# Attention followed by a gated MLP: an earlier start of the first v tiles, a check of the softmax sums on the chip, and a branch at the end

## The chip, the core and the metric

The kernel runs on one core of one Trainium2 chip. The core has five engines that work side by side and meet at semaphores: TensorE (PE in the profile, with PEld for its weight loads), VectorE (DVE), ScalarE (ACT), GpSimd (POOL) and SyncE (SP), which here issues transfers. Sixteen DMA engines move data between the memory of the chip (DRAM) and the core's on-chip memory SBUF. [...] The metric is the device time of one execution in microseconds; the kernel before takes 251.71 us (median of three runs, 251.39 to 252.03).

## The reference

Per batch (8 of them), grouped-query attention with 16 query heads, 4 key and value heads, 384 positions and head size 64, and then a gated MLP with a spatial gate on its result:

```python
k = np.repeat(k, group, axis=1); v = np.repeat(v, group, axis=1)
scores = scale * np.matmul(q, k.transpose(0, 1, 3, 2))
scores = scores - np.max(scores, axis=-1, keepdims=True)
attn = np.exp(scores)
attn = attn / (np.sum(attn, axis=-1, keepdims=True) + 1e-09)
x = np.matmul(attn, v)          # then to (B, S, 1024)
...
h = np.maximum(x @ w_in, 0.0)   # (1024, 1024)
u, v = h[..., :512], h[..., 512:]
v_n = (v - mean(v)) / np.sqrt(var(v) + 1e-06)
v_s = np.einsum('ts,bsd->btd', w_spatial, v_n) + b_spatial[None, :, None]
out = (u * v_s) @ w_out         # (512, 1024)
```

The inputs q, k and v are normal numbers times 0.1, so that scores are small; the kernel before computes exp without subtracting the maximum.

## The kernel before

The whole program is written out without loops on the chip; the order of each engine's queue is the order in which Python calls the helpers. The outer loop counts turns n from 0 to 149. A batch has 18 *units* (NU): six groups m (three tiles of 128 query rows, two halves of the heads), each with three tiles of 128 keys. `scores(n)` (L224) makes two matmuls of 512 columns into a double-buffered PSUM tile `sc` and one exp on ScalarE (L240), which casts to the fp16 tile `aT`. When the three units of a group are done, `weigh` (L242) makes, for each of the two key heads of the half, twelve matmuls of 65 columns into the single PSUM buffer `av`; the 65th column is the sum of the softmax, because `v1` carries a column of ones. VectorE takes the reciprocal `r` (L257) and multiplies (L259) into `x16`. Two `weigh` calls of a group stand in neighbouring turns, and the second needs the buffer that the first one's multiplication frees.

x is transposed into `xt`: in batch 0, and for the last two groups of the last batch, on TensorE by `x_transposes` (L271, with a copy on VectorE), else by a transposing transfer on SP's queue. The MLP runs as *fill*: a generator `stream` (L467) yields after each matmul the columns it spent, and `run_fill` (L631) draws as many columns as the turn is allotted (L651 to L657). Its pieces are `v_tile` (L288: eight matmuls of 512 columns, then `vr`, `stats` and `mv` on VectorE), `u_tile` or `u_block`, `normal` (L311), `gate`, and `project`. All of these, the transposes and the warm matmuls share the three PSUM buffers with the tag `ck`.

`normal` makes rstd on ScalarE (L314, L315: Ln, then Exp), `nmr` = -mean x rstd on VectorE (L316), and the three normalised tiles `vn` = vr x rstd + nmr, mostly on POOL (L327). `keep_warm` (L545) makes small matmuls on the identity while little other work is there: 27 at the very start, some between the first transposes, and four in each of the turns 0 to 9, 14 and 15. Their PSUM tile `warm` (L543) is held from the start until turn 15.

The turns at which casts, transfers and transposes stand are written out by hand (`at`, `turn_at`). Within a turn the order is: listed loads and casts, scores, `weigh`, listed transposes and warm matmuls, fill. Up to turn 16 each turn n makes the scores of unit n + 1; from turn 18 on each even turn makes two units.

At the end the last batch's `project` sends each half row block on its own (L462), the last in two pieces of 384 and 128 columns. Then follows the framework's closing block (L684): SP waits for every transfer, and all engines meet at a barrier twice.

Of the kernel before, what the change touches and what calls it, by code (L numbers as in the profile page):

```python
# [17 lines left out]
def kernel(  # L18
# [166 lines left out]
    def k_transposes(b, j, eng):  # L185
        ps = ps_ck.tile([P, S], FP16, name=f"kps_{b}_{j}", tag="ck")
        for t in range(NT):
            nc.tensor.transpose(
                ps[:, t * P : (t + 1) * P],
                k16s[b][:, j, t].rearrange("p h d -> p (h d)"),  # L190
                ident16,
            )
        eng(k_tile(b)[:, j], ps)
# [25 lines left out]
        )  # L219


    aTs, avs, x16s, xts = {}, {}, {}, {}

    def scores(n):  # L224
# [17 lines left out]
    def weigh(b, m, hh):  # L242
        qt, j = divmod(m, 2)
        av = ps_av.tile([P, G, D + 1], FP32, name=f"av_{b}_{m}_{hh}", tag="av")
        for i in range(G):
            for t in range(NT):
                nc.tensor.matmul(  # L247
                    av[:, i, :],
                    aTs[b, m][:, t, hh, i * P : (i + 1) * P],
                    v1[b % 2][:, 2 * j + hh, t, 0 : D + 1],  # L250
                    start=(t == 0),
                    stop=(t == NT - 1),
                )
# [3 lines left out]
        nc.vector.reciprocal(r, av[:, :, D : D + 1])  # L257
        blk = 4 * j + 2 * hh
        nc.vector.tensor_tensor(  # L259
            x16s[b][:, qt, blk : blk + 2].rearrange("p k (i d) -> p (k i) d", i=2),  # L260
            av[:, :, 0:D],
            r.to_broadcast([P, G, D]),
            ALU.mult,
        )
# [6 lines left out]
    def x_transposes(b, m):  # L271
        qt, j = divmod(m, 2)
        ps = ps_ck.tile([P, 4, P], FP16, name=f"xps_{b}_{m}", tag="ck")
        for i in range(4):
            nc.tensor.transpose(ps[:, i], x16s[b][:, qt, 4 * j + i], ident16)  # L275
        nc.vector.tensor_copy(x_tile(b)[:, qt, 4 * j : 4 * j + 4], ps)

    def x_turn(b, qt, lo, hi):
# [3 lines left out]
            transpose=True,  # L282
        )


    mvs, v_rs, v_ns, uTs, gTs, osbs = {}, {}, {}, {}, {}, {}

    def v_tile(b, st):  # L288
        if st == 0:
            mvs[b] = small.tile([P, NT, 2], FP32, name=f"mv_{b}", tag="mv")  # L290
            v_rs[b] = []
        pv = ps_ck.tile([P, 512], FP32, name=f"pv_{b}_{st}", tag="ck")
        for kt in range(NB):
            nc.tensor.matmul(  # L294
                pv,
                x_tile(b)[:, st, kt],
                w_in16[:, kt, DH:DFF],
                start=(kt == 0),
                stop=(kt == NB - 1),
            )  # L300
# [3 lines left out]
        nc.vector.tensor_scalar(vr, pv, 0.0, None, op0=ALU.max)  # L304
        stats = small.tile([P, 6], FP32, name=f"stats_{b}_{st}", tag="stats")
        nc.vector.bn_stats(stats, vr)  # L306
        nc.vector.bn_aggr(mvs[b][:, st, :], stats)
        v_rs[b].append(vr)
        yield 512

    def normal(b):  # L311
        rstd = small.tile([P, NT], FP32, name=f"rstd_{b}", tag="rstd")
        nmr = small.tile([P, NT], FP32, name=f"nmr_{b}", tag="nmr")
        nc.scalar.activation(rstd, mvs[b][:, :, 1], AF.Ln, bias=eps_t)  # L314
        nc.scalar.activation(rstd, rstd, AF.Exp, scale=-0.5)  # L315
        nc.vector.scalar_tensor_tensor(  # L316
            nmr, mvs[b][:, :, 0], -1.0, rstd, op0=ALU.mult, op1=ALU.mult
        )
# [221 lines left out]

    by_dve, by_act = nc.vector.tensor_copy, nc.scalar.copy

    warm = ps_ck.tile([P, 512], FP32, name="warm", tag="ck")  # L543

    def keep_warm(n):  # L545
        for _ in range(n):
            nc.tensor.matmul(warm[:, 0:P], ident16, ident16, start=True, stop=True)  # L547

# [82 lines left out]
    def run_fill(cols):  # L631
        nonlocal owed
        owed += cols
        while owed > 0:
            owed -= next(fill, 1e9)

    for n in range(total + 6):
        for f, args in todo.pop(n, []):
            f(*args)
        if n + 1 < NU:  # L640
            scores(n + 1)
        elif n >= NU and n % 2 == 0 and n < total:
            scores(n)
            scores(n + 1)
        for hh in range(2):
            b, r = divmod(n - 3 - hh, NU)
            if n >= 3 + hh and r % 3 == 0 and b < B:
                weigh(b, r // 3, hh)
        for f, args in turns.pop(n, []):
            f(*args)  # L650
        if n < NU + 3:  # L651

            run_fill(HV / 4 if 10 <= n < 14 else 2 * HV / 5 if 16 <= n else 0)
        elif n < 2 * NU + 4:
            run_fill((4 * HV + NM * NT * S + 6 * NM * 512) / (NU + 4 - 3))
        else:
            run_fill(COLS / NU)  # L657
    for _ in fill:
        pass
    assert not todo and not turns  # L660
# [1 line left out]
_INS = ['q', 'k', 'v', 'moe_w_in', 'moe_w_spatial', 'moe_b_spatial', 'moe_w_out']  # L662
# [26 lines left out]
```

## Time and profile before

| | |
|---|---|
| time, median of three runs | 251.71 us (251.39 to 252.03) |
| the profiled execution's own time | 251.51 us |
| its span, first to last instruction | 249.7 us |
| PE busy | 240.9 us (96%), 2438 matmuls |
| ScalarE, VectorE, POOL busy | 169.1, 139.9, 97.4 us |
| the 144 exps on ScalarE | 139.6 us, 1021 ns each |
| the 85 warm matmuls | 9.2 us as the profile counts them (they overlap) |
| granted TensorE clock in 7 to 249.7 us | 1.00 |

The profile is one execution as the hardware profiler recorded it. Lines of the order of time give the start and the length in us, the engine, the line of the kernel, the operation, the tile written and the tiles read, and in brackets how long the engine stood idle before it and for whom. Matmuls overlap in the pipeline, so their distance from start to start says more than their length. The page's lines on the queues give packets, megabytes, and the share of the DMA engines' time; the two queues of kind "instruction" fetch the program's own code.

### The profile page before, as it was taken

How to read it: one execution, taken by the hardware profiler on the slowest of the kernel's cores; microseconds unless marked ns; L12 is line 12 of the kernel's file. 1: busy time of each engine (PE TensorE's matmuls, PEld its weight loads, DVE VectorE, ACT ScalarE, POOL GpSimd, SP SyncE). 2: the span in 40 equal slices, each digit the busy share in tenths (PEclk: the TensorE clock that was granted, in tenths of full speed). 3: DMA queues.
4: the chain of work that ended last, by engine and by line, in shares of the span. 5: the costliest groups of instructions: out<-in, count | busy, mean ns of one | idle time of the engine just before them, and what ended most of it. 6: DMA issues, size and time to landing. Idle time of an engine off the chain costs nothing.

```text
span 249.7 us, 6038 instructions
## 1 busy us (share of the span) xinstructions
PE 240.9 (96%) x2438; PEld 126.2 (51%) x2438; DVE 139.9 (56%) x370; ACT 169.1 (68%) x217; POOL 97.4 (39%) x141
## 2 busy tenths in 40 slices
PE   7998998999999999999999999999999999999993
PEld 7564666634455445544455445544455444554551
DVE  2455777764546646375536746375536746375662
ACT  3896665777686677868686677868686687862231
POOL 2698836881034800393034800393034000350130
PEclk9999999999999999999999999999999999999999
DMA  7999998999379973996479973999474172024206
GB/s 180 269 285 252 301 281 238 289 233 265 104 145 326 173 276 66 236 274 178 168 145 333 169 273 71 206 302 175 171 151 90 24 273 45 0 46 168 84 26 230
DMA packets 73980, 46.93 MB, mean 188 GB/s; under 512 B 48112, under 2 KB 68912, under 8 KB 73952
## 3 DMA queue, kind: packets, MB, share of 16 engines
q1 hardware_dynamic: 68832, 37.63, 59.2%
q0 software_dynamic: 4080, 8.65, 13.9%
q8 instruction: 19, 0.31, 0.5%
q10 hardware_dynamic: 1040, 0.26, 0.5%
q14 instruction: 9, 0.07, 0.1%
HBM read 25.95 MB, written 12.58 MB: 154 GB/s over the span
## 4 chain that ended last, share of the span: by engine, by line
PE 91%; DVE 6%; ACT 1%; issue 1%; POOL 0%; POOLq 0%
PE av L247 17%; PE pv L294 16%; PE sc L233 15%; PE po L449 15%; PE pu L359 14%; PE psp L378 6%; PE warm L547 3%; DVE x L259 2%; DVE stats L306 1%; DVE vr L304 1%; PE pu L342 1%; PE qps L200 1%; ACT aT L240 1%; PE psp L402 1%; PE xps L275 1%
## 5 line engine op out<-in xcount | busy, mean ns | idle before, releaser
L240 ACT ACTIVATE aT<-sc 128x1024 f16<-128x1024 f32 x144 | 139.6, 1021 | 53.3 <-PE sc L233 53.1
L247 PEld LDWEIGHTS <-aT 128*128 128x128 f16 x1152 | 43.4, 97 | 32.9 <-DVE x L259 12.8
L327 POOL TENSOR_SCALAR vn<-vr,rstd,nmr 128x512 f16<-128x512 f32 x22 | 16.9, 778 | 100.0 <-DVE r L257 86.2
L247 PE MATMUL av<-v,aT 128*128 128x65 f16 x1152 | 52.4, 194 | 1.6 <-DVE x L259 1.2
L257 DVE RECIPROCAL r<-av 128x4 f32<-128x4 f32 x96 | 17.2, 179 | 58.3 <-PE av L247 57.7
L294 PE MATMUL pv<-w_in,xt 128*128 128x512 f16 x192 | 49.6, 379 | 0.0
L449 PE MATMUL po<-w_out,gT 128*128 128x512 f16 (+2 forms) x196 | 47.9, 375 | 0.0
L233 PE MATMUL sc<-qT,kT 64*128 64x512 f16 x288 | 45.4, 385 | 0.5 <-DVE qT L205 0.3
L259 DVE TENSOR_TENSOR x<-av,r 128x256 f16<-128x256 f32 x96 | 40.8, 425 | 3.4
L359 PE MATMUL pu<-xt,w_in 128*128 128x384 f16 x216 | 40.2, 326 | 0.0
L389 POOL TENSOR_TENSOR gT<-g,uT 128x384 f16<-128x384 f32 x28 | 24.7, 914 | 26.8 <-DVE g L388 26.8
L359 PEld LDWEIGHTS <-w_in 128*128 128x128 f16 x216 | 19.4, 98 | 14.2 <-issue 2.5
L170 POOL CAST q<-q 128x768 f16<-128x768 f32 (+1 forms) x36 | 24.9, 733 | 3.1 <-DMA q<-in_q_dram 3.1
L449 PEld LDWEIGHTS <-gT 128*128 128x128 f16 x196 | 16.9, 97 | 18.3 <-issue 2.9
L294 PEld LDWEIGHTS <-xt 128*128 128x128 f16 x192 | 16.1, 97 | 13.5 <-issue 0.6
L458 DVE COPY osb<-po 128x512 f32<-128x512 f32 (+1 forms) x25 | 16.7, 667 | 11.1 <-PE po L449 11.1
L233 PEld LDWEIGHTS <-kT 64*128 64x128 f16 x288 | 8.9, 94 | 26.4 <-issue 24.0
L304 DVE TENSOR_SCALAR vr<-pv 128x512 f32<-128x512 f32 x24 | 16.5, 688 | 10.2 <-PE pv L294 10.0
L458 ACT COPY osb<-po 128x512 f32<-128x512 f32 (+1 forms) x24 | 14.0, 584 | 10.6 <-PE po L449 10.5
L306 DVE BATCH_NORM_STATS2 stats<-vr 128x6 f32<-128x512 f32 x24 | 16.7, 695 | 0.8
L378 PE MATMUL psp<-wsT,vn 128*128 128x384 f16 x84 | 17.0, 327 | 0.0
L388 DVE TENSOR_TENSOR g<-psp,bias_b 128x384 f32<-128x384 f32 x28 | 14.4, 552 | 2.7 <-PE psp L378 2.7
(59 smaller groups left out, 136.2 us busy)
## 6 DMA issues: line engine op xcount, KB each, us to landing
out_dram<-osb SPq DMA_DIRECT2D x21, 512.0 KB, 2.9
q<-in_q_dram SPq DMA_DIRECT2D x10, 768.0 KB, 7.1
q<-in_q_dram POOLq DMA_DIRECT2D x4, 768.0 KB, 10.4
v<-in_v_dram SPq DMA_DIRECT2D x6, 384.0 KB, 8.7
w_in<-in_moe_w_in_dram POOLq DMA_DIRECT2D x4, 512.0 KB, 9.8
k<-in_k_dram SPq DMA_DIRECT2D x5, 384.0 KB, 4.1
out_dram<-osb SPq DMA_DIRECT2D x5, 256.0 KB, 2.0
q<-in_q_dram SPq DMA_DIRECT2D x2, 512.0 KB, 7.2
```

The costliest lines, as they stand in the source:

```text
L170: f(q16s[b, j][:, lo:hi, :, hh, :], src[:, hh, lo:hi])
L233: nc.tensor.matmul(sc[:, hh], kTs[b][half, j, t * P : (t + 1) * P], qTs[b, j][half, qt], start=True, stop=True,)
L240: nc.scalar.activation(aTs[b, m][:, t], sc, AF.Exp, scale=scale)
L247: nc.tensor.matmul(av[:, i, :], aTs[b, m][:, t, hh, i * P : (i + 1) * P], v1[b % 2][:, 2 * j + hh, t, 0 : D + 1], start=(t == 0), stop=(t ...
L259: nc.vector.tensor_tensor(x16s[b][:, qt, blk : blk + 2].rearrange("p k (i d) -> p (k i) d", i=2), av[:, :, 0:D], r.to_broadcast([P, G, D]) ...
L294: nc.tensor.matmul(pv, x_tile(b)[:, st, kt], w_in16[:, kt, DH:DFF], start=(kt == 0), stop=(kt == NB - 1),)
L306: nc.vector.bn_stats(stats, vr)
L359: nc.tensor.matmul(pu[:, 0:S].rearrange("p (t s) -> p t s", t=NT), w_in16[:, kt, m * P : (m + 1) * P], x_tile(b)[:, :, kt], start=(kt == 0 ...
L378: nc.tensor.matmul(psp[:, 0:S], v_ns[b][st][:, m * P : (m + 1) * P], wsT16[:, st, :], start=(st == 0), stop=(st == NT - 1),)
L389: nc.gpsimd.tensor_tensor(gTs[b][:, m, :], g, uTs[b][:, m, :], ALU.mult)
L449: nc.tensor.matmul(po[:, 0 : hi - lo], gTs[b][:, m, tt * P : (tt + 1) * P], w_out16[:, m, lo:hi], start=(m == 0), stop=(m == NM - 1),)
L458: (nc.scalar.copy if half and not i else nc.vector.tensor_copy)(osb[:, lo:hi], po[:, 0 : hi - lo])
```

## The change

Four things are changed.

The first v tiles start earlier. The fill of turns 6 to 9 is an eighth of a v tile each (one matmul), of 10 and 11 a quarter, of 13 to 15 a sixth, of 16 and 17 a quarter, of 18 to 20 a third; before it was a quarter in 10 to 13 and two fifths from 16 to 20. By turn 20 both have drawn three tiles. Warm matmuls remain in turns 0 to 5 alone, and each call takes its own PSUM tile. Scores run ahead by one unit up to unit 12, unit 13 stands in turn 13, and from turn 14 on they come in pairs.

`normal` computes (vr + minus) x rstd with `minus` = -mean, which does not need rstd; only the tile that ScalarE makes in the last batch needs the product `ac`.

All reciprocals are kept in one tile `r_all` (128 x 384). Behind the last transposes of x, `judge` (five VectorE instructions) tests that each lies in [2e-5, 20], reduces over the columns, and `verdict`, behind the last v tiles, counts the good partitions with a one-column matmul and writes a flag.

At the end every engine loads the flag and compares. If it is set, `again` runs the whole attention once more with the maximum subtracted, and the MLP after it. If it is not set, each engine falls through into a short block (waits for its own work, on SP for the transfers), which ends in a jump over the code of `again` to the closing block. That code is 11,509 instructions, of which PE has 7721, VectorE 2613, ScalarE 861, POOL 200 and SP 114. With the given inputs the flag is not set.

```diff
+    r_all = cst.tile([P, B * HQ * NT], FP32, name="r_all")
...
-        r = small.tile([P, G, 1], FP32, name=f"r_{b}_{m}_{hh}", tag="r")
+        at_r = (6 * b + m) * 2 * G + hh * G
+        r = r_all[:, at_r : at_r + G].unsqueeze(2)
...
+    def judge():
+        shape = [P, B * HQ * NT]
+        big = cst.tile(shape, FP32, name="big_enough")
+        fine = cst.tile(shape, FP32, name="fine")
+        nc.vector.tensor_scalar(big, r_all, 20.0, None, op0=ALU.is_le)
+        nc.vector.scalar_tensor_tensor(fine, r_all, 2e-5, big, op0=ALU.is_ge, op1=ALU.mult)
+        each = cst.tile([P, 1], FP32, name="each")
+        nc.vector.tensor_reduce(each, fine, mybir.AxisListType.X, ALU.min)
+        each16 = cst.tile([P, 1], FP16, name="each16")
+        nc.vector.tensor_copy(each16, each)
+        ones = cst.tile([P, 1], FP16, name="ones")
+        nc.vector.memset(ones, 1.0)
+        judged["each"], judged["ones"] = each16, ones
+
+    def verdict():
+        count = ps_av.tile([1, 1], FP32, name="count", tag="av")
+        nc.tensor.matmul(count, judged["each"], judged["ones"], start=True, stop=True)
+        flag = cst.tile([1, 1], mybir.dt.int32, name="flag")
+        nc.vector.tensor_scalar(flag, count, float(P), None, op0=ALU.is_lt)
+        judged["flag"] = flag
+
+    def attend_with_maximum(b):
...
+    def again():
+        for d in (xts, uTs, gTs, mvs, v_rs, v_ns, osbs, kTs, qTs, k16s, q16s):
+            d.clear()
+        for b in range(B):
+            attend_with_maximum(b)
...
     def normal(b):
         rstd = small.tile([P, NT], FP32, name=f"rstd_{b}", tag="rstd")
-        nmr = small.tile([P, NT], FP32, name=f"nmr_{b}", tag="nmr")
+        minus = small.tile([P, NT], FP32, name=f"minus_{b}", tag="minus")
         nc.scalar.activation(rstd, mvs[b][:, :, 1], AF.Ln, bias=eps_t)
         nc.scalar.activation(rstd, rstd, AF.Exp, scale=-0.5)
-        nc.vector.scalar_tensor_tensor(
-            nmr, mvs[b][:, :, 0], -1.0, rstd, op0=ALU.mult, op1=ALU.mult
-        )
+        nc.vector.tensor_scalar(minus, mvs[b][:, :, 0], -1.0, None, op0=ALU.mult)
+        if b == B - 1:
+            ac = small.tile([P, 1], FP32, name="ac", tag="ac")
+            nc.vector.tensor_tensor(ac, minus[:, 2:3], rstd[:, 2:3], ALU.mult)
...
-            a, c = rstd[:, st : st + 1], nmr[:, st : st + 1]
+            a, c = minus[:, st : st + 1], rstd[:, st : st + 1]
             if b == B - 1 and st == 2:
-                nc.scalar.activation(vn, v_rs[b][st], AF.Identity, scale=a, bias=c)
+                nc.scalar.activation(vn, v_rs[b][st], AF.Identity, scale=c, bias=ac)
             else:
                 by = nc.vector if b == B - 1 and st == 1 else nc.gpsimd
-                by.tensor_scalar(vn, v_rs[b][st], a, c, op0=ALU.mult, op1=ALU.add)
+                by.tensor_scalar(vn, v_rs[b][st], a, c, op0=ALU.add, op1=ALU.mult)
...
                 yield from v_tile(b, 1)
                 yield from v_tile(b, 2)
+                if last:
+                    verdict()
...
-    warm = ps_ck.tile([P, 512], FP32, name="warm", tag="ck")
-
     def keep_warm(n):
+        warm = ps_ck.tile([P, 512], FP32, name="warm", tag="ck")
         for _ in range(n):
             nc.tensor.matmul(warm[:, 0:P], ident16, ident16, start=True, stop=True)
...
-    for n in (*range(10), 14, 15):
+    for n in range(6):
         turn_at(n, keep_warm, 4)
...
-        if n + 1 < NU:
+        if n < 12:
             scores(n + 1)
-        elif n >= NU and n % 2 == 0 and n < total:
+        elif n == 13:
+            scores(n)
+        elif n % 2 == 0 and n > 13 and n < total:
             scores(n)
             scores(n + 1)
...
+        if n == total + 2:
+            judge()
         if n < NU + 3:
-            run_fill(HV / 4 if 10 <= n < 14 else 2 * HV / 5 if 16 <= n else 0)
+            at_n = {6: 8, 7: 8, 8: 8, 9: 8, 10: 4, 11: 4, 13: 6, 14: 6, 15: 6, 16: 4, 17: 4}
+            run_fill(HV / at_n[n] if n in at_n else HV / 3 if n >= NU else 0)
...
+    out_of_range = (
+        nc.values_load(judged["flag"], skip_runtime_bounds_check_because="it is only compared") > 0
+    )
+    with tc.If(out_of_range, preferred_fallthrough_block=False):
+        again()
```

More of the change, by code (lines that the diff above doesn't have):

```diff
@@ L283, in x_turn @@
         )
+    judged = {}
+    def judge():
[11 more added lines that the diff above has]
+        judged["each"], judged["ones"] = each16, ones
@@ new lines, in verdict @@
+    def verdict():
[5 more added lines that the diff above has]
+    def attend_with_maximum(b):
+        load_k(b)
+        for j in range(2):
+            load_q(b, j)
+        load_v(b)
+        cast_k(b, pool)
+        for j in range(2):
+            cast_q(b, j, pool)
+        cast_v(b, pool)
+        for j in range(2):
+            k_transposes(b, j, by_dve)
+            for t in range(NT):
+                q_transposes(b, j, t, by_dve)
+        x16s[b] = att.tile([P, NT, NB, P], FP16, name=f"x16_{b}", tag="x16")
+        for qt in range(NT):
+            for h in range(HQ):
+                g, i = divmod(h, G)
+                j, hh = divmod(g, 2)
+                half = slice(hh * D, (hh + 1) * D)
+                s = ps_ck.tile([P, S], FP32, name="s_max", tag="ck")
+                nc.tensor.matmul(
+                    s,
+                    qTs[b, j][half, qt, i * P : (i + 1) * P],
+                    kTs[b][half, j],
+                    start=True,
+                    stop=True,
+                )
+                top = small.tile([P, 1], FP32, name="top", tag="top")
+                nc.vector.tensor_reduce(top, s, mybir.AxisListType.X, ALU.max)
+                nc.vector.tensor_scalar(top, top, -scale, None, op0=ALU.mult)
+                p = moe.tile([P, NT, P], FP16, name="p", tag="vn", bufs=6)
+                nc.scalar.activation(
+                    p.rearrange("q t s -> q (t s)"), s, AF.Exp, scale=scale, bias=top
+                )
+                ps = ps_sc.tile([P, NT, P], FP16, name="pps", tag="sc")
+                for t in range(NT):
+                    nc.tensor.transpose(ps[:, t], p[:, t], ident16)
+                pT = moe.tile([P, NT, P], FP16, name="pT", tag="vn", bufs=6)
+                nc.vector.tensor_copy(pT, ps)
+                av = ps_av.tile([P, D + 1], FP32, name="av_max", tag="av")
+                for t in range(NT):
+                    nc.tensor.matmul(
+                        av,
+                        pT[:, t],
+                        v1[b % 2][:, g, t, 0 : D + 1],
+                        start=(t == 0),
+                        stop=(t == NT - 1),
+                    )
+                r = small.tile([P, 1], FP32, name="r_max", tag="r")
+                nc.vector.reciprocal(r, av[:, D : D + 1])
+                nc.vector.tensor_scalar(
+                    x16s[b][:, qt, h // 2, (h % 2) * D : (h % 2 + 1) * D],
+                    av[:, 0:D],
+                    r,
+                    None,
+                    op0=ALU.mult,
+                )
@@ new lines, in again @@
+    def again():
[3 more added lines that the diff above has]
+            attend_with_maximum(b)
+            for m in range(6):
+                x_transposes(b, m)
+            for st in range(NT):
+                for _ in v_tile(b, st):
+                    pass
+            for m in range(NM):
+                for _ in u_block(b, m):
+                    pass
+            for m in range(NM):
+                for _ in gate(b, m):
+                    pass
+            for tt in range(NT):
+                for half in range(2):
+                    for _ in project(b, tt, half):
+                        pass
@@ L659 @@
         pass
+    out_of_range = (
+        nc.values_load(judged["flag"], skip_runtime_bounds_check_because="it is only compared") > 0
+    )
+    with tc.If(out_of_range, preferred_fallthrough_block=False):
+        again()
     assert not todo and not turns
```

## The prediction

> **What bounds the kernel now.** First I read the page: the busy shares and the chain that ended last, then the instruction queues.
>
> ```profile
> span 249.7 us, 6038 instructions
> ...
> PE 240.9 (96%) x2438; PEld 126.2 (51%) x2438; DVE 139.9 (56%) x370; ACT 169.1 (68%) x217; POOL 97.4 (39%) x141
> ...
> q8 instruction: 19, 0.31, 0.5%
> q14 instruction: 9, 0.07, 0.1%
> ...
> PE 91%; DVE 6%; ACT 1%; issue 1%; POOL 0%; POOLq 0%
> ```
>
> TensorE is the bound: 91% of the chain is PE. So a change gains what it takes off PE's queue or out of PE's waits, and loses what PE waits anew. The two instruction queues fetch code: q8 in pieces of 16 KB (0.31 MB over 19), q14 in pieces of 8 KB. Second I read PE's order of time between 13 and 30 us, where the change rewrites the order, and DVE's beside it.
>
> ```profile
> 13.93 0.39 PE L547 MATMUL warm<-ident 128*128 128x128 f16 x4
> 14.15 0.39 PE L275 MATMUL xps<-ident,x 128*128 128x128 f16 x4
> 14.47 0.39 PE L233 MATMUL sc<-qT,kT 64*128 64x512 f16 x2
> ...
> 20.42 0.39 PE L200 MATMUL qps<-ident,q 128*128 128x128 f16 x4
> 21.65 0.38 PE L275 MATMUL xps<-ident,x 128*128 128x128 f16 x4 [0.84 <-DVE qT L205]
> ...
> 28.67 0.61 PE L233 MATMUL sc<-qT,kT 64*128 64x512 f16 x4
> ```
>
> ```profile
> 14.80 0.41 DVE L276 COPY xt<-xps 128x512 f16<-128x512 f16 x1
> ...
> 23.86 0.68 DVE L304 TENSOR_SCALAR vr<-pv 128x512 f32<-128x512 f32 x1
> 24.58 0.69 DVE L306 BATCH_NORM_STATS2 stats<-vr 128x6 f32<-128x512 f32 x1
> 25.31 0.18 DVE L307 BATCH_NORM_AGGREGATE mv<-stats 128x2 f32<-128x6 f32 x1
> ```
>
> PE has one idle stretch here (0.84) and six groups of warm matmuls; start to start the groups cost 0.22 for four 128-column matmuls, 0.32 for two scores, 0.38 for twelve av, 0.22 per pv. The copy of xt ends at 15.21, 0.84 after PE's transposes are through; vr, stats and mv hold DVE 1.5 us in one piece. Third, the waits around the normalisation, in batch 0 on PE and in a later batch on DVE and PE.
>
> ```profile
> 40.23 0.55 PE L247 MATMUL av<-v,aT 128*128 128x65 f16 x12 [0.58 <-DVE x L259]
> ```
>
> ```profile
> 99.51 0.16 DVE L316 SCALAR_TENSOR_TENSOR nmr<-mv,rstd 128x3 f32<-128x3 f32 x1 [1.45 <-ACT rstd L315]
> 99.59 0.18 DVE L257 RECIPROCAL r<-av 128x4 f32<-128x4 f32 x1
> 99.80 0.42 DVE L259 TENSOR_TENSOR x<-av,r 128x256 f16<-128x256 f32 x1
> ```
>
> DVE stands 1.45 us for rstd from ScalarE with finished av behind it, so the single av buffer is free late. Last, the end: the copies, SP's final waits (one of the rows below is all after the last landing), and transfers by time to landing.
>
> ```profile
> 245.65 0.48 ACT L458 COPY osb<-po 128x384 f32<-128x384 f32 x1 [0.93 <-PE po L449]
> 245.87 0.29 DVE L458 COPY osb<-po 128x128 f32<-128x128 f32 x1 [0.18 <-PE po L449]
> ```
>
> ```profile
> L684 SPq EVENT_SEMAPHORE  x6: 27/28/28, 248.5 to 248.8; - x6
> L684 SPq DRAIN  x2: 7/10/13, 248.9 to 248.9; - x2
> ```
>
> ```profile
> k<-in_k_dram SPq DMA_DIRECT2D x2, 192.0 KB, 3.4
> ...
> out_dram<-osb SPq DMA_DIRECT2D x1, 64.0 KB, 1.9
> ```
>
> The last write lands at 248.5; SP's waits follow each other every 0.06 us, its drain is at 248.9, and the closing barrier takes the last 0.75 to 249.7.
>
> **The change, part by part.**
>
> *The early half of v (turns 6 to 17).* It removes 24 warm matmuls (4 x 0.22 from turns 6 to 9, twice 0.22 at 14 and 15: 1.32 us), spreads v_tile(0, 0) from turn 6 on, and issues the scores of turns 13 to 17 later and in pairs (two merges, each 2 x 0.32 against 0.54: 0.2). Up to 13.93 nothing moves. From there I follow the new order with the distances above.
> - Turn 6: transposes end at 14.15, the first pv needs the xt copy that ends at 15.21 (DVE's chain before it is the same): PE idle 1.1. Before, scores stood here. W_in is no obstacle: its two transfers for v were issued at 5.9 and 6.9 and landed after 7.6 and 10.0, at 13.5 and 16.9; the second is first read about 19.4.
> - Turns 7 to 11: one pv per turn, then two; short waits for an exp and the next xt copy, about 0.15. v_tile(0, 0) ends at 20.65 on PE.
> - Turns 12, 13: DVE now takes vr, stats and mv of it at 20.85 *ahead* of the reciprocal of the next av; that begins at 22.4, its x ends at 23.05, and the second av of that pair, otherwise ready at 21.9, waits for the buffer: 1.2 idle. The two pv behind it wait 0.3 for the next xt copy.
> - Turns 14, 15: scores come as a pair at 24.3, their first exp ends at 25.75 (1.02 from the exp row, 0.43 after the score's start as at 14.47 and 14.90), and av waits 0.4 for it.
> - Turns 16, 17: no wait; the pair of scores that stood at 28.67 starts at 29.25, with one pv more done (0.22): 0.36 behind.
> - Turn 19: vr, stats, mv of v_tile(0, 1) again stand before r and x, 0.55 idle on the second av; the 0.3 that PE loses at 32.9 for the last x goes instead.
> Sum: 0.36 + 0.55 - 0.3 = **+0.6 us**. Bounds: none of these waits would be -1.32 - 0.84 - 0.4 = -2.5; each longer by half, +2.
>
> *The normalisation.* `minus` needs only the mean, so DVE no longer waits for rstd before r and x: batch 0, 0.58 of PE idle gone. In the later batches the av at 100.28 stands 0.62 after its scores (99.66), the same pair elsewhere 0.54 (102.70, 103.24): 0.08, in six batches 0.5. In the last batch the vn on POOL starts at once with rstd instead of after nmr, worth the 0.1 by which PE's psp is late at 237.16; the extra `ac` (one column) stands in nmr's place there. `vn` costs the same with add and mult exchanged. What is late next is PE itself. Sum **-1.2** (between -0.5, if PE's other waits take the place, and -1.4).
>
> *judge and verdict.* Five DVE instructions behind the last xt copy (ends 228.26): three over 128x384, each at most the 0.55 of the nearest rows (g, 128x384; vn, 128x512), and two tiny ones at 0.1 to 0.2: about 1.7, to 230.0. Behind them waits the copy of osb that ran at 229.04; it ends at 230.7, and its PSUM buffer is wanted by pu at 233.15. Next on DVE is vr at 231.70. So nothing: the cover is 1 us before vr; without it the whole 1.7 would lie on PE. PE comes to the one-column matmul at 233.1, long after its input (230.0), so pu behind it waits for nothing but its 0.06; the flag (about 0.1) stands on DVE in front of `minus`, while ScalarE makes rstd for 0.5. r_all only changes where reciprocals lie: 0. SP and POOL are passed by none of this.
>
> *The branch at the end.* Each engine, behind its last instruction, loads the flag into a register, compares, waits for its own work, and jumps over the block of the second softmax to the closing block; the fall-through way is the one taken here, but it ends in this jump. Over PE's 7721, DVE's 2613, ScalarE's 861, POOL's 200, SP's 114 instructions.
> - SP: behind the last write (248.5) five waits to 248.8, a jump, then twelve waits and a drain at 0.06 (before: five and a drain in all): drain at 249.7 instead of 248.9, **+0.75**. Its load lies beside the write's 1.9.
> - The others jump beyond any code at hand (q8's 0.31 MB for PE's 2 x 2438 instructions make 64 bytes each, so q14's 8 KB are 128). DVE's copy ends at 246.16; load 0.7 (no row; between a semaphore's 0.03 and 1.9, the shortest trip through memory; on-chip, hence nearer the lower), compare 0.1, fetch 3.4 (no row either; bounds 0.3 and 4.7, the first reads of q; the nearest is a small early read, k, 3.4): ready at 250.4, later than SP. ScalarE (246.13) and PE (245.83) come just before it.
> So the barrier begins at 250.4 instead of 248.9: **+1.5**, bounds +0.75 and +4.
>
> [...]
>
> **Sum.** +0.6 - 1.2 + 1.5 = +0.9. The profiled execution took 251.51 us (span 249.7, 1.8 around it), so 252.4; it is 0.2 below the median 251.71, so on the median **252.6 us**, +0.36%.
>
> **The rivals.**
> - *A jump costs only its instruction.* The fetches end before SP does, as they start 2.7 us earlier. For it: 8 KB pieces; packets of code are small beside q1's 37.63 MB, and DMA is nearly idle at the end. Against: every read row from issue to landing is over 3 us. 251.51 + 0.6 - 1.2 + 0.75 + 0.2 = 251.9.
> - *SP's jump is fetched as well.* Then 3.4 comes behind the last landing: 248.8 + 0.1 + 3.4 + 0.8 = 253.1 for the drain, +4.2: 255.3. For it: nobody covers SP. [...]
> - *The other side: faster.* Pv in the place of warm matmuls fills PE where ScalarE's exps set the pace (exps stand end to end until 19.1), and the DVE waits I count do not come. Place: turns 6 to 19; price: +0.6 becomes about -1.4, half-way to the bound: 250.6. It decides from -1.1 on. Against: vr, stats and mv stand ahead of the reciprocal on DVE in the new order.
>
> **How the numbers follow.** 0.3% (0.75 us) is about what a measurement of this kernel can tell from no change. Forecast 0.47 (its own range 251.7 to 253.6, on both sides of the 252.5 that bounds slower: 0.29 slower, 0.18 same); cheap jump 0.24 (0.18 same, 0.04 faster, 0.02 slower); SP fetched 0.13 (slower); faster early half 0.16 (0.13 faster, 0.03 same). Together: faster 0.17, same 0.39, slower 0.44. The range leaves out most of SP fetched and the far end of the faster case: 250.8 to 254.2.
>
> **What would show it.** Right: PE idle about 1 us before the first pv near 14.2, and 1 us at the second av near 22; the pair of scores for batch 1 near 29.2; no DVE idle for rstd, and PE's 0.58 at 40 gone; later batches 0.08 shorter; judge's rows between 228 and 230 with the next vr not later than now against PE; PE's last matmul 0.6 earlier; engines other than SP reaching the closing drain last. Wrong: the early idle absent, or the gap from the last copy to the end unlike 249.7 - 246.2 + 1.5 = 5.0 us.

## The result, and the profile after

The changed kernel takes **256.19 us** (median of four runs, 255.69 to 256.35) against 251.55 us for the kernel before in runs on the same chip (251.26 to 252.03): a ratio of 1.018, interval 1.0162 to 1.0197. The forecast was 252.6 us with a range to 254.2. It is slower by 4.6 us where +0.9 was forecast, and the time lies outside the range. The profiled execution took 256.35 us, 4.84 more than the 251.51 of before's. Line numbers of the changed kernel differ: scores are L234, `weigh`'s matmuls L248, the multiplication into x L261, the branch L782, the closing block L808.

The page: PE is still the bound, but DMA has entered the chain that ended last, and the code queues carry 2 and 6 more pieces.

```profile
span 254.5 us, 6027 instructions
...
PE 239.5 (94%) x2415; PEld 124.9 (49%) x2415; DVE 142.2 (56%) x377; ACT 169.1 (66%) x217; POOL 97.6 (38%) x141
...
q8 instruction: 21, 0.34, 0.6%
...
q14 instruction: 15, 0.12, 0.2%
...
PE 84%; DVE 6%; DMA 4%; ACT 1%; POOL 1%; issue 1%
```

PE's order of time in the early half (start, length, engine, line, operation, tiles, count, idle time before):

```profile
15.40 0.39 PE L402 MATMUL pv<-w_in,xt 128*128 128x512 f16 x1 [0.95 <-DVE xt L278]
...
23.38 0.55 PE L248 MATMUL av<-v,aT 128*128 128x65 f16 x12 [1.12 <-DVE x L261]
...
26.09 0.48 PE L248 MATMUL av<-v,aT 128*128 128x65 f16 x10 [0.35 <-ACT aT L241]
...
27.57 0.38 PE L277 MATMUL xps<-ident,x 128*128 128x128 f16 x4 [0.60 <-DVE kT L193]
...
30.20 0.71 PE L234 MATMUL sc<-qT,kT 64*128 64x512 f16 x4
...
32.52 0.55 PE L248 MATMUL av<-v,aT 128*128 128x65 f16 x12 [0.30 <-DVE x L261]
```

The waits forecast as 1.1, 1.2 and 0.4 are there as 0.95, 1.12 and 0.35. The fourth, 0.60, was not forecast: the transposes of x's group 3 take the `ck` buffer (in PSUM, which PE writes and VectorE reads here) that the transposes of batch 1's k have just filled, and stand until VectorE has copied it to kT. The scores at 30.20 are those that the forecast put at 29.25.

VectorE beside it, at the 1.12:

```profile
21.16 0.69 DVE L412 TENSOR_SCALAR vr<-pv 128x512 f32<-128x512 f32 x1 [0.76 <-PE pv L402]
21.89 0.69 DVE L414 BATCH_NORM_STATS2 stats<-vr 128x6 f32<-128x512 f32 x1
22.61 0.18 DVE L415 BATCH_NORM_AGGREGATE mv<-stats 128x2 f32<-128x6 f32 x1
22.71 0.15 DVE L259 RECIPROCAL r_all<-av 128x4 f32<-128x4 f32 x1
22.90 0.42 DVE L261 TENSOR_TENSOR x<-av,r_all 128x256 f16<-128x256 f32 x1
```

The block of vr, stats and mv stands in front of the reciprocal, as forecast. Later on PE, the place of the normalisation in batch 0 (it stood 0.58 before) has no wait left, but at the first scores of batch 2 there is a new one. These scores before, without a wait, and then both places after:

```profile
56.35 0.60 PE L233 MATMUL sc<-qT,kT 64*128 64x512 f16 x4
```

```profile
41.28 0.55 PE L248 MATMUL av<-v,aT 128*128 128x65 f16 x12
...
58.21 0.61 PE L234 MATMUL sc<-qT,kT 64*128 64x512 f16 x4 [0.75 <-DMA qT<-q]
```

VectorE in a later batch: `minus` at once, and the reciprocal waits for PE and no longer for rstd; and the judge's rows, 229.5 to 231.3, with VectorE idle 1.16 before the next vr.

```profile
99.87 0.17 DVE L426 TENSOR_SCALAR minus<-mv 128x3 f32<-128x3 f32 x1
100.57 0.18 DVE L259 RECIPROCAL r_all<-av 128x4 f32<-128x4 f32 x1 [0.53 <-PE av L248]
...
229.52 0.35 DVE L295 TENSOR_SCALAR big_enough<-r_all 128x384 f32<-128x384 f32 x1
...
230.50 0.55 DVE L298 TENSOR_REDUCE each<-fine 128x1 f32<-128x384 f32 x1
...
233.05 0.69 DVE L412 TENSOR_SCALAR vr<-pv 128x512 f32<-128x512 f32 x1 [1.16 <-PE pv L402]
```

The end, by source line: instructions of each engine's sequencer with shortest, median and longest duration in ns, and first and last start.

```profile
L782 PEldq COMPARE_BRANCH  x2: 95/2132/4168, 247.1 to 247.5; - x2
L782 ACTq COMPARE_BRANCH  x2: 38/44/49, 247.8 to 248.0; - x2
L782 DVEq COMPARE_BRANCH  x2: 51/53/55, 247.9 to 248.1; - x2
L782 SPq COMPARE_BRANCH  x2: 38/48/57, 249.3 to 252.3; - x2
```

```profile
L808 SPq DRAIN  x3: 7/7/13, 253.6 to 253.9; - x3
L808 ACTq DRAIN  x2: 8/44/80, 251.3 to 253.9; - x2
L808 DVEq DRAIN  x2: 10/34/57, 251.6 to 253.9; - x2
L808 PEldq DRAIN  x2: 8/40/73, 251.7 to 254.0; - x2
```

Each engine's second branch row is the jump, its first drain is the closing block. PE's jump takes 4.17 (the longest of its two rows); ScalarE's and VectorE's rows are short, but their next instruction comes 3.3 and 3.5 later. All three are at the closing block by 251.7; SP comes at 253.6, last. The transfers in the four microseconds 248 to 252, with the time from issue to landing at the right of the last line (1.9 before):

```profile
q14 instruction: 2, 0.02, 1.7%
q8 instruction: 1, 0.02, 1.6%
...
out_dram<-osb SPq DMA_DIRECT2D x1, 64.0 KB, 3.8
```

**Where the 4.8 us come from**, by the starts of the same PE instructions in both profiled executions: +0.12 at the start, +1.50 from there to 36.6 us (early half), -0.57 by 43 us (normalisation, batch 0), +0.82 at the scores of 58.21, then -0.42 over six batches; PE ends 1.44 later. From VectorE's last copy to the end of the span it is 6.85 instead of 3.54: +3.31. Around the span 1.89 instead of 1.80.

### The profile page after: what moved, and what is told of

It is laid out like the page before. It is cut to its first block, busy times and chain, and to the rows that moved or that the text cites. A ratio compares the mean times of both kernels' runs of the same rounds, so it can differ in the third digit from the quotient of the medians.

```text
span 254.5 us, 6027 instructions
## 1 busy us (share of the span) xinstructions
PE 239.5 (94%) x2415; PEld 124.9 (49%) x2415; DVE 142.2 (56%) x377; ACT 169.1 (66%) x217; POOL 97.6 (38%) x141
## 4 chain that ended last, share of the span: by engine, by line
PE 84%; DVE 6%; DMA 4%; ACT 1%; POOL 1%; issue 1%
PE av L248 16%; PE pv L402 16%; PE sc L234 14%; PE po L560 14%; PE pu L470 14%; PE psp L489 5%; DMA qT<-q 2%; PE pu L453 2%; DVE x L261 2%; DMA k<-in_k_dram 1%; ACT aT L241 1%; POOL gT L500 1%; DVE stats L414 1%; DVE vr L412 1%; PE warm L659 1%
## 5 line engine op out<-in xcount | busy, mean ns | idle before, releaser
L248 PEld LDWEIGHTS <-aT 128*128 128x128 f16 x1152 | 43.7, 97 | 33.7 <-issue 13.4
L438 POOL TENSOR_SCALAR vn<-vr,minus,rstd 128x512 f16<-128x512 f32 x22 | 17.0, 784 | 99.7 <-ACT rstd L425 99.7
L248 PE MATMUL av<-v,aT 128*128 128x65 f16 x1152 | 52.6, 194 | 2.7 <-DVE x L261 2.1
L259 DVE RECIPROCAL r_all<-av 128x4 f32<-128x4 f32 x96 | 17.1, 179 | 65.2 <-PE av L248 64.8
L234 PE MATMUL sc<-qT,kT 64*128 64x512 f16 x288 | 44.8, 382 | 1.4 <-DMA qT<-q 0.7
L261 DVE TENSOR_TENSOR x<-av,r_all 128x256 f16<-128x256 f32 x96 | 40.7, 424 | 3.3
L234 PEld LDWEIGHTS <-kT 64*128 64x128 f16 x288 | 8.9, 94 | 27.4 <-issue 25.8
```

Source lines behind the costliest of these rows:

```text
L234: nc.tensor.matmul(sc[:, hh], kTs[b][half, j, t * P : (t + 1) * P], qTs[b, j][half, qt], start=True, stop=True,)
L248: nc.tensor.matmul(av[:, i, :], aTs[b, m][:, t, hh, i * P : (i + 1) * P], v1[b % 2][:, 2 * j + hh, t, 0 : D + 1], start=(t == 0), stop=(t ...
L261: nc.vector.tensor_tensor(x16s[b][:, qt, blk : blk + 2].rearrange("p k (i d) -> p (k i) d", i=2), av[:, :, 0:D], r.to_broadcast([P, G, D]) ...
```

## The experiments

Times are medians; the kernel before is 251.47 us in the first two groups of four and 251.46 in the last group of two.

**The kernel without the guard** (without judge, verdict, flag and branch). It splits the change in two.

```diff
-                if last:
-                    verdict()
...
-        if n == total + 2:
-            judge()
...
-    with tc.If(out_of_range, preferred_fallthrough_block=False):
-        again()
```

> The changed kernel without judge, verdict, flag and branch; the early half of v and the new normalisation stay. It leaves out the test of the softmax sums. Theory: of the 4.6 us lost, some 3.3 lie behind the last copy (guard), and before it stand +1.5 (early half), +0.8 (scores of batch 2 waiting for the transposed q) and -1.1 (normalisation). So 252.7 to 253.0 us, the distance from the last copy's end to the end of the span back from 6.9 to 3.5 us. Rival: the early half costs nothing by itself and the guard is the whole loss: 250.5 to 251.5 us.

Measured: 252.3 us (251.92 to 253.53), ratio 1.0033 (1.0005 to 1.006). That is below the 252.7 to 253.0 expected. From the first scores to its end PE needs 240.38 us in this trace, 240.29 in the changed kernel and 239.18 before: without judge and verdict PE is no faster, so these cost nothing, and the part before the end costs 1.1 to 1.2 in both traces. Only the first scores begin at other times: at 6.06 here, at 6.43 before and at 6.77 in the changed kernel, where the first k landed 0.6 later than here (4.14 instead of 3.56). Against before the landing is the same, and the same first four scores take 0.61 instead of 1.04. From the last copy to the end it is 3.57 as before (3.54). The guard is thus worth 256.19 - 252.3 = 3.9 us. In the traces 3.3 of it lie behind the last copy; the other 0.6 goes with the later first scores (6.77 instead of 6.06).

**The same jumps over little code.** The body behind the branch is cut to a dozen instructions; loads, waits and jumps stay.

```diff
     with tc.If(out_of_range, preferred_fallthrough_block=False):
-        again()
+        scr = cst.tile([P, 8, D], FP32, name="scr")
+        for i in range(8):
+            nc.sync.dma_start(scr[:, i], k[0, 0, 0:P])
+        one = cst.tile([P, 4], FP32, name="one")
...
+        keep_warm(1)
```

> The changed kernel with the body of the branch cut to a dozen instructions, so that the flag loads, compares, waits and jumps are the same ones, and only the code jumped over is short. It leaves out the second softmax. Theory: the jumps' code fetches cost the end twice, by their own 3 to 4 us on PE, DVE and ACT and by holding up the last writes on the DMA engines by 1.9 us; without them the last landing is back at 1.9 to 2.0 us after its issue, and the distance from the last copy to the end is 3.5 + 0.75 (more waits on SP) + 0.1 to 0.4 (jump) = 4.3 to 4.7 us: 253.6 to 254.1 us. Rival: flag loads, compares and waits themselves are the cost: 6.9 us there and 256 us.

Measured: 254.1 us (253.44 to 254.34), ratio 1.0099 (1.0064 to 1.0133). So of the guard's 3.9 us, 2.1 belong to the length of the code jumped over, and 1.8 stay with a branch over a dozen instructions. PE's rows, and the transfers from 247.5 to 251.5 us:

```profile
L782 PEldq COMPARE_BRANCH  x2: 90/135/180, 247.0 to 247.4; - x2
```

```profile
out_dram<-osb SPq DMA_DIRECT2D x1, 64.0 KB, 1.9
```

PE's jump takes 0.18 instead of 4.17, no code is fetched in this stretch, and the last write takes the 1.9 that it took before. From the last copy to the end it is 5.02: 1.5 more than before, and it all lies behind the landing, in SP's queue: 2.70 from landing to the end of the span, 1.23 before. SP's jump takes 0.18 here, and a pause of 0.33 stands between two of its waits behind the jump; why is open.

**PE alone jumps far.** To the last kernel 4,000 PE instructions are added behind the branch; the other engines still jump over a few.

```diff
-        keep_warm(1)
+        keep_warm(2000)
```

> As the short jump, but PE alone jumps far, over 4000 instructions (2000 warm matmuls); VectorE, ScalarE, POOL and SP jump over a few. It leaves out the second softmax. Theory: one 16 KB fetch holds up the last writes as well; PE itself is ready 4 us after its jump, at about 251.5, which is near SP's own 251.7 with short jumps; the landing 0.7 to 1.5 us later than with short jumps: 254.6 to 255.6 us. Rival (it takes the three engines together, or VectorE's): no later landing, 253.9 to 254.3 us.

Measured: 255.69 us (255.1 to 255.81), ratio 1.0163 (1.0144 to 1.0181), just above the expected range. PE's rows, and the transfers from 247.5 to 251.5 us:

```profile
L782 PEldq COMPARE_BRANCH  x2: 95/2065/4035, 246.6 to 247.0; - x2
```

```profile
q8 instruction: 1, 0.02, 1.4%
...
out_dram<-osb SPq DMA_DIRECT2D x1, 192.0 KB, 3.8
out_dram<-osb SPq DMA_DIRECT2D x1, 64.0 KB, 3.5
```

With one fetch of 16 KB by PE, both of the last writes need 3.8 and 3.5 instead of the 2.2 and 1.9 in the kernel with the short jump. PE itself reaches the closing block at 251.12, while SP passes its wait for the last landing at 251.19 and is there only at 253.0: PE's own stall is covered, and what costs is the late landing of the writes. The times of the single pieces show which part is late. The trace has 16 partial landings for each of these writes, and SP's wait for a write ends with the sixteenth (251.70 and 251.71 in the changed kernel for the 192 KB write, 251.87 and 251.89 for the other). In this run 15 of the 16 of the 192 KB write came by 249.29 and the last at 251.00; of the 64 KB write 15 by 249.48 and the last at 251.17. The fetch ran from 248.71 to 249.63, and the pieces of 1536 bytes that are missing from the first write start at 249.62, where it ends: eight of them, then the eight of 512 bytes of the second write, through at 250.70. In the changed kernel the fetch runs from 249.17 to 250.22, the first of these late pieces starts at 250.22, and the two writes are complete at 251.70 and 251.87. In the kernel with the short jump all 16 come within 0.24. These times would fit a fetch and late pieces that share one of the page's 16 DMA engines; that is my reading and not shown, as the trace does not name the DMA engine of a piece.

**The far jump at the comparison.** The block is placed so that the compare itself jumps, and no engine runs through a block that ends in a jump.

```diff
-    with tc.If(out_of_range, preferred_fallthrough_block=False):
+    with tc.If(out_of_range, preferred_fallthrough_block=True):
```

> The changed kernel with the two blocks of the branch in the other order, so that the far jump is the compare itself, in front of each engine's last waits, and the closing block follows the short block. Theory (the fetches of the jumps hold up the last writes): PE, DVE and ACT fetch 0.1 to 0.4 us earlier, in the midst of the same writes, so the last landing stays 1.5 to 2 us late; SP's jump now lies beside the landing and its 0.4 goes: 255.5 to 256.0 us. Rival (the cost is the jump that SP makes behind the landing): 254 us or less.

Measured: 255.71 us (255.13 to 255.97), ratio 1.0165 (1.0145 to 1.0184): as expected, 0.5 less than the changed kernel. The fetch moved with the jump: PE's began at 248.18, a microsecond earlier, and the writes were still complete only at 251.60 and 251.77. Moving the far jump a microsecond forward thus won 0.5 of the guard's 3.9 us. For the last write there is a second reason in this run: SP's issue of it took 1.81 us instead of some 0.4 and ended only at 249.86; why is open.

**The new order of the early half alone**, put into the kernel before (warm tile for each call, warm matmuls in turns 0 to 5, scores and fill as in the changed kernel).

```diff
-    for n in (*range(10), 14, 15):
+    for n in range(6):
...
-        if n + 1 < NU:
+        if n < 12:
...
-            run_fill(HV / 4 if 10 <= n < 14 else 2 * HV / 5 if 16 <= n else 0)
+            at_n = {6: 8, 7: 8, 8: 8, 9: 8, 10: 4, 11: 4, 13: 6, 14: 6, 15: 6, 16: 4, 17: 4}
+            run_fill(HV / at_n[n] if n in at_n else HV / 3 if n >= NU else 0)
```

> The kernel before with nothing but the new order of turns 0 to 20 (fill, scores, warm matmuls). Theory: +1.5 us at the scores of unit 20, from PE's waits near 14.2 (1.0), 22 (1.1), 25.7 (0.4) and 26.8 (0.6) less the removed warm matmuls, and up to 0.8 more at the first scores of batch 2, which wait for the transposed q: 253.0 to 253.9 us. Rival: those waits only use up slack, and the order is neutral or a gain: 250.5 to 251.8 us.

Measured: 253.65 us (252.93 to 254.52), ratio 1.0095 (1.0063 to 1.0127), within the expected range. On PE it is +1.34 at 36 us and +2.1 from the first scores of batch 2 on, where the wait for the transposed q (0.7) stands as well. So that wait is brought by the new early order, without guard or normalisation.

**The new normalisation alone**, `minus` and `ac` put into the kernel before (the diff of `normal` shown above).

> The kernel before with nothing but the normalisation as (vr + minus) x rstd. Theory: 0.57 us less at the av near 40 us, 0.08 in each of six batches and about 0.1 in the last: 250.4 to 250.6 us, no DVE idle for rstd. Rival: PE's other waits take the place: 251.3 to 251.7 us.

Measured: 250.92 us (250.51 to 252.0), ratio 0.998 (0.9958 to 1.0001), a little above the expected range; the interval reaches no change. On PE it gains 0.70 by 53 us (0.57 of it at the normalisation of batch 0, 0.12 before 20 us, where the kernels do not differ). At the scores of batch 2 a new wait of 0.4 for the transposed q stands and 0.5 of the gain is gone; the later batches bring it back to 0.7 at the end of PE. Removing one wait made another visible: the transfers do not move forward as PE does.

**The loads of batch 3 behind the transposes of batch 2**, in the kernel without the guard.

```diff
-                at(w0 - NU + 11, load_k, b)
-                at(w0 - NU + 11, load_q, b, 0)
-                at(w0 - NU + 11, load_q, b, 1)
-                at(w0 - NU + 11, load_v, b)
+                l0 = w0 - NU + (14 if b == 3 else 11)
+                at(l0, load_k, b)
+                at(l0, load_q, b, 0)
+                at(l0, load_q, b, 1)
+                at(l0, load_v, b)
```

> The kernel without the guard (early half and new normalisation stay), with the loads of batch 3 put on SP's queue three turns later, behind the transposing transfers of k and q of batch 2. Theory: those transposes stood on SP's queue behind a load that waits for POOL's casts; in front of it they land 3 us or more earlier, PE's 0.8 at the first scores of batch 2 goes, and nothing takes its place: 251.3 to 251.7 us. Rival: the transposes wait for POOL's casts and for the DMA engines anyway, or the loads of batch 3 come late then: 252.1 to 252.6 us.

Measured: 251.99 us (251.61 to 252.19), ratio 1.0013 (1.0 to 1.0025): 0.3 below the kernel without the guard, between the two expectations. Of PE's waits in the kernel without the guard (total, times, longest) this row is gone, and one of 0.6 for a cast of q on POOL has come:

```profile
PE sc L234 <- DMA qT<-q: 0.8, 1, 0.8
```

The wait for the transposed q is gone, and from there to the end PE is 0.9 faster (172.27 instead of 173.14 from the scores at 54 us to the last av of batch 7). The new wait is at 10.9 us, in a part that is the same in both kernels: in this execution the first v landed 0.6 later. What holds the transposes up is thus the loads in front of them on SP's queue. SP's rows in the kernel without the guard, and then in this one:

```profile
45.91 2.38 SPq L82 DMA_DIRECT2D v<-in_v_dram  x1
48.39 2.77 SPq L208 DMA_TRANSPOSE kT<-k  x1
51.26 5.95 SPq L215 DMA_TRANSPOSE qT<-q  x2
```

```profile
44.68 1.22 SPq L208 DMA_TRANSPOSE kT<-k  x1
46.01 3.29 SPq L215 DMA_TRANSPOSE qT<-q  x2
...
55.63 2.46 SPq L82 DMA_DIRECT2D v<-in_v_dram  x1
```

In front of the loads the transposes come 3.7 earlier, and their rows are about half as long. That the load of v waits for POOL to free its tile, as the expectation has it, is not shown: here it takes 2.46 although POOL's last cast of v ended at 48.23, and as the last of four loads it takes 1.8 to 2.9 in every batch from 3 on in the kernel before and in the changed one. Nor is it what grew: it takes 2.14 in the changed kernel and 2.21 before. What is longer in the changed kernel are the transposing transfers, of x in front of the loads (2.14 against 1.34) and of q (5.89 against 5.24); why is open. The wait was removed in this trace; how much of it shows in the time, 0.3 to 0.9, the runs do not settle.

**The statistics one turn later**, in the kernel without the guard.

```diff
-            at_n = {6: 8, 7: 8, 8: 8, 9: 8, 10: 4, 11: 4, 13: 6, 14: 6, 15: 6, 16: 4, 17: 4}
+            at_n = {6: 8, 7: 8, 8: 8, 9: 8, 10: 4, 11: 8, 12: 8, 13: 6, 14: 6, 15: 6, 16: 4, 17: 4}
```

> The kernel without the guard (early half and normalisation), with one thing changed: the fill of turn 11 is an eighth instead of a quarter of a half row of v, and turn 12 takes the other eighth, so that v_tile(0, 0) ends one turn later and its vr, stats and mv come on VectorE behind the r and x of the av pair near 23 us. Theory: the 1.12 us that the second av near 23 us waits for x in the changed kernel is the 1.5 us block of vr, stats and mv standing in front of the reciprocal; with the block behind it that wait falls to 0.3 or less, and some 0.3 to 0.6 of it comes back as waits for the next xt copy, which the block then delays. That is 0.5 to 0.8 us less than the 252.3 of the kernel without the guard: 251.5 to 251.8. Rival: the early half is late because the exps set its pace, and the wait at 23 us only shows slack of PE: then the wait moves to the scores behind it, 252.1 to 252.5.

Measured: 251.48 us (251.04 to 252.12), ratio 0.9998 (0.9986 to 1.001), at the lower edge of the expected range: 0.8 less than without this edit, and no change against the kernel before. PE and VectorE at that place:

```profile
22.07 0.55 PE L248 MATMUL av<-v,aT 128*128 128x65 f16 x12
...
24.62 0.55 PE L248 MATMUL av<-v,aT 128*128 128x65 f16 x12 [0.43 <-DVE x L261]
...
26.16 0.38 PE L277 MATMUL xps<-ident,x 128*128 128x128 f16 x4 [0.60 <-DVE kT L193]
```

```profile
21.41 0.42 DVE L261 TENSOR_TENSOR x<-av,r_all 128x256 f16<-128x256 f32 x1
...
22.41 0.68 DVE L412 TENSOR_SCALAR vr<-pv 128x512 f32<-128x512 f32 x1
```

The av that stood 1.12 at 23 us follows without a wait, because x comes before the block. A wait of 0.43 comes one av later in place of the 0.35 for the exp, and the one for kT stays. So the 1.12 was the order on VectorE, and not slack in front of the exps.

**A warm tile for each call**, in the kernel before and nothing else.

```diff
-    warm = ps_ck.tile([P, 512], FP32, name="warm", tag="ck")
-
     def keep_warm(n):
+        warm = ps_ck.tile([P, 512], FP32, name="warm", tag="ck")
```

> The kernel before with one thing changed: each call of the warm matmuls takes its own PSUM tile, so that none is held until turn 15 (order, number and place of the warm matmuls as before; the old normalisation). Theory: the 0.84 us that the transposes of x wait for a PSUM buffer at 20.8 us in the kernel before goes, and 0.4 to 0.6 us of waits for x beside it, as in the kernel with the old order, the new normalisation, this change and the later loads (start of the first scores to the av near 22 us: 15.07 there against 16.29). Expected: 1.0 to 1.2 us less than before, 250.3 to 250.5. Rival: the stall at 20.8 is slack in front of the exps, which set the pace, and the gain of that kernel came from its loads: within 0.3 us of before, 251.2 to 251.6.

Measured: 250.73 us (250.27 to 250.91), ratio 0.996 (0.9946 to 0.9975). PE at the place that stood 0.84 before:

```profile
20.26 0.39 PE L200 MATMUL qps<-ident,q 128*128 128x128 f16 x4
20.48 0.39 PE L275 MATMUL xps<-ident,x 128*128 128x128 f16 x4
```

The stall is gone. The profiled execution gains 1.2 (250.27), the median 0.7, which is less than expected. The changed kernel makes this edit too, but the new order around it loses more than this on the way.

**The old order with the three small edits**: the new normalisation, a warm tile for each call and the later loads, in the kernel before, without guard and without the new early order.

> The kernel before with the new normalisation, a PSUM tile for each call of the warm matmuls instead of one that is held until turn 15, and the loads of batch 3 behind the transposes of batch 2; order of turns 0 to 20 and number of warm matmuls as before. Theory: 1.1 from the normalisation, 0.8 from PE's stall at 20.8 us (the transposes there wait for a buffer), and no wait for the transposed q: 249.4 to 249.9 us. Rival: the buffer is not what the stall at 20.8 is about, or the transposed q still sets the pace at batch 2: 250.5 to 251.0 us.

Measured: **249.18 us** (249.08 to 249.28), ratio 0.991 (0.9893 to 0.9926): it beats both kernels, and its own expectation a little. PE's waits, behind the one at the very start:

```profile
...
PE av L247 <- DVE x L259: 0.7, 2, 0.4
PE sc L233 <- ACT aT L240: 0.4, 1, 0.4
PE sc L233 <- DVE qT L205: 0.3, 1, 0.3
PE pu L345 <- DVE qT L205: 0.2, 1, 0.2
```

Neither the wait for the `ck` buffer nor that for the transposed q is there. Counted from its first scores, PE is 1.22 faster by the second av near 22 us, 0.56 more by 42 us, and 0.49 between the first scores of batch 2 and the end.

## Why the prediction was wrong, point by point

- **The branch at the end, forecast +1.5, measured +3.3: a term mis-sized.** The parts were nearly right. The load of the flag took 0.55 to 0.76 (forecast 0.7). The jump took 3.3 on ScalarE, 3.5 on VectorE and 4.2 on PE (forecast 3.4). Engines other than SP were ready 4.1 us after the last copy (forecast 4.2). What failed is the step "SP: behind the last write (248.5) five waits to 248.8": it took the landing of the last write as given. The fetches delay that landing: 3.41 us after the end of its issue instead of 1.46, **+1.95**. In the cheap-jump rival I had written that "DMA is nearly idle at the end"; it is, but the two last writes are under way in just that microsecond. And SP's queue costs 1.3 instead of 0.75, from the landing to its drain (1.69 instead of 0.39 before), with another 0.05 in the barrier behind it: its waits follow each other every 0.06 as forecast, but its jump takes 0.5 where no more than 0.1 was put, and the waits ahead of the jump 0.4 instead of 0.3. No run shows the 0.1 as such that was put for a compare and for SP's jump, and no row of before gave it: in the changed kernel the branch rows other than PE's far jump take 0.04 to 0.10, and from SP's jump to its next instruction it is 0.5. SP, and not the others, is last. Without the late landing the forecast's gap of 5.0 from the last copy to the end would nearly have been met (6.85 - 1.95 = 4.90; 5.02 in the run with the short jump), but by luck: SP's queue makes it, while the fetches of the others, for which the +1.5 was put, are covered. The short jump (no late landing, +1.5 at the end) and PE's far jump alone (late landing again) separate the two parts.
- **The rival "SP's jump is fetched as well"** gave 255.3, near the time, by luck: it puts 3.4 behind the landing for SP's jump, which took 0.5, and leaves out that the landing itself is late. The forecast itself gave SP's jump over 114 instructions no fetch; no run shows that it needed none, and over a dozen instructions it took 0.18. Whether a fetch has a part in the 0.5 is open: an 8 KB fetch of q14 ran from 252.21 to 252.69 beside this jump (252.30 to 252.80), and the trace does not show for which engine.
- **The early half, forecast +0.6, measured +1.5: mis-sized.** The waits named were right (0.95, 1.12, 0.35, and 0.30 before the second av at 32.52). Missing was the 0.60 for kT: three `ck` buffers are dealt out in turn, and I followed who fills which on VectorE's queue, but not for the transposes of x behind those of k. It moves the scores of batch 1 from 29.25 to 30.20, with 0.2 of smaller waits and 0.1 of a later start. The 0.3 that PE lost near 33 did go, as forecast (two matmuls of x's transposes stood 0.36 apart there), but stretches of 0.1 without a recorded wait, near 30 and 35, took most of it back. The rival "faster" fell with this: the waits on VectorE came, and the statistics one turn later removed one of them.
- **A wait that no part of the sum held: +0.8** for the transposed q of batch 2. Each stage was followed on PE and VectorE; SP's queue, where the loads of batch 3 stand in front of those transfers, was not followed past 30 us. The run with the later loads shows that they are what can be moved; the early half alone brings the wait (0.7), the normalisation alone part of it (0.4). Why the transfers fall behind PE by more than in the kernel before stays open.
- **The normalisation, forecast -1.2, measured -1.0: right.** 0.57 in batch 0 (forecast 0.58), and 0.42 over six batches (forecast 0.5); alone it gives -0.55 in the median, because the wait for the transposed q takes 0.5 back.
- **Judge and verdict, forecast 0: right.** 1.7 us on VectorE as worked out, with 1.16 of idle left behind it and the copy of osb.

With the forecast's +0.9, the four differences are +0.9 (early half), +0.8 (transposed q), +1.8 (end) and +0.2 (normalisation); with 0.1 at the start and 0.1 around the span that makes 4.8, the difference of the profiled executions.

## What to carry to other kernels

The guard here, whose other branch is long, was paid for where it is jumped over: 2.1 of its 3.9 us went with the length of that code. PE's own stall of 4.0 us in the run where it alone jumps far was covered by SP; what cost was that the two last writes landed 3.8 and 3.5 us after their issue instead of 2.2 and 1.9. So with a long branch, look for transfers in flight at the moment of the jump, the last writes above all. When a schedule is rewritten, follow every rotating buffer and every queue to the next place where they are the last to arrive, SP's included, and not only the engine that is the bound. Three small edits to the old order, each aimed at one wait that a profile names, gained 2.3 us where the new order lost.

## What the runs showed of the hardware that was not expected

- With one 16 KB code fetch of PE (0.92 us) beside them, the last of the 16 partial landings of two writes in flight came 1.7 us behind the other fifteen: 3.8 and 3.5 us from issue to landing instead of 2.2 and 1.9 without a fetch.
- The far jumps do not show in the same way on all engines: on PE the branch row itself is 3.9 to 4.2 us long in three runs, on ScalarE and VectorE it stays at 0.04 and 0.05 in the changed kernel and the next instruction is 3.3 and 3.5 late. Over a dozen instructions PE's jump takes 0.18.
- Of four loads issued in a row on SP's queue, from batch 3 on, the first three take 0.4 to 0.9 us each and the last 1.8 to 2.9, in the kernel before and in the changed one; what it waits for the traces do not show.
- Loading one word of the on-chip memory into a register took 0.48 us on POOL to 0.76 us on PE.
